# Two gaps between the operands of the first layer: where columns and weights begin in SBUF

## The chip, the cores and the metric

The kernel runs on one core of one Trainium2 chip. The metric is the device time of one execution in microseconds; the figure for a kernel is the median of its runs. One further execution is taken with the hardware profiler, and all views of the profile are of that one.

## What is computed

The reference first makes a short causal convolution over time (7 taps, weights from a softmax, one set of taps for each of 8 heads), and then a layer pair with a hard-swish between:

```python
out = np.einsum('hk,bskhg->bshg', w, x_unf)   # (8, 4096, 192), 7 taps
h = x @ w_in                                  # (32768, 192) @ (192, 2048)
relu6 = np.clip(h + 3.0, 0.0, 6.0)
g = h * relu6 / 6.0
return (g @ w_out).astype(np.float32)         # (32768, 2048) @ (2048, 192)
```

## The kernel before

The 32768 tokens are worked in 32 blocks of 1024 tokens. In each block the convolution gives `y`, the first layer gives `g`, and the second layer gives 192 outputs for each token. The work of the next block's convolution and of the sums for the second layer is laid between by hand (`tc.manual_schedule()`, with lists of jobs and due times), so the order on each engine is the order of the program.

**First layer.** A block's 1024 tokens are two groups of 512 columns; the 192 inputs are 3 thirds of 64 rows. Rows 0-63 of a tile hold the lower group, rows 64-127 the upper one. `y` is split into a high and a low part, `y_own[HIGH]` and `y_own[LOW]` (tiles `y0` and `y1`), and `swap_parts` copies them with DMAs of SP into `y_other`, where the two halves of the rows are exchanged. The weights are split in the same way into `w_in0` and `w_in1`. A product is made in three passes:

```python
PASSES = (HIGH, HIGH), (LOW, HIGH), (HIGH, LOW)   # (weights, columns)
```

One unit `n` of 16 makes 128 of the 2048 hidden features for both token groups: 3 passes x 3 thirds x 2 halves of the rows, 18 matmuls (`products`, L442), each 64 rows x 128 weight columns x 512 columns of `y`. The two matmuls of a pair stand in different halves of the array's rows. Units 0 to 7 read the own parts, units 8 to 15 the exchanged ones (in the first block they alternate). ScalarE (`relu`, L315) and VectorE (`gate`, L319) then turn a unit's two PSUM banks into `g`; four such pairs of banks go round.

In all this makes 32 blocks x 16 units x 9 pairs = 4608 pairs of matmuls. The operands are bitcast to float32r.

**Second layer.** It is a two-level Strassen-like scheme in plain float32, each matmul 128 rows x 32 weight columns x 512 or 256 columns, on four column groups of the array side by side (L582; the first block uses `direct_chunk`, L330, instead). `plain` puts a 512-column matmul at 2 units of a column group's list, `small` puts a 256-column one at 1 unit; at the point where the rest is added, the code asserts `clock[q] == 44`. Among its moving operands are `g`, sums of it (`s1`, `s3` and others), `z`, the early sums in the slots of `y0` and `y1` (`z0`, `z1`), and `z_other` in the slot of `y_other`. `pe_tap` (L923) makes a part of the first block's convolution on TensorE, with 128 x 128 weights.

**Places in SBUF.** A pool gives its tiles addresses one behind the other, in the order in which they are first asked for; pools stand in the order in which they are opened (`cst`, `xs`, `ys`, `yo`, `ot`, and others behind them). In `cst` stand, among others, `g`, then `w_in0`, `w_in1`, `w_out`; in `yo` stand `sm`, `y0`, `y1` and the tile with the tag `other`. In bytes in each partition, a third of `y` takes 2048, a part 6144, and the 128 weight columns of a matmul 512.

Of the kernel before, what the change touches and what calls it, by code (L numbers as in the profile page):

```python
# [11 lines left out]
F32 = mybir.dt.float32  # L12
# [8 lines left out]
HIGH, LOW = range(2)  # L21
# [10 lines left out]
def kernel(  # L32
# [9 lines left out]
    P = nc.NUM_PARTITIONS  # L42
# [6 lines left out]
    N = 512  # L49
# [3 lines left out]
    K3 = D // D2  # L53
# [7 lines left out]
    NP = NC // 2  # L61
# [5 lines left out]
    cst = ctx.enter_context(tc.tile_pool(name="cst", bufs=1))  # L67
    xs = ctx.enter_context(tc.tile_pool(name="xs", bufs=1))
    ys = ctx.enter_context(tc.tile_pool(name="ys", bufs=1))
    yo = ctx.enter_context(tc.tile_pool(name="yo", bufs=1))  # L70
# [48 lines left out]
    nc.vector.memset(zeros, 0.0)  # L119


    w_in_parts = [cst.tile([P, NP, K3, P], F32, name=f"w_in{n}") for n in range(2)]
    def own_tiles(name):
        return [yo.tile([P, K3, N], F32, name=f"{name}{n}", tag=f"y{n}") for n in range(2)]

    sm = yo.tile([P, 1], F32, name="sm")
    y_own, z_early = own_tiles("y"), []

    def other_tile():
        return yo.tile([P, 2, K3, N], F32, name="y_other", tag="other")  # L130

    y_other = [other_tile()]
    w_out = cst.tile([P, NP, 7, DH], F32, name="w_out")
    B11, B12, B21, B22, T1, T2, T4 = range(7)
# [99 lines left out]
    def r32(ap):  # L234
        return ap.bitcast(F32R)
# [39 lines left out]
    y = ys.tile([P, K3, N], F32, name="y")  # L275
# [26 lines left out]
    def swap(to, part):  # L302
        nc.sync.dma_start(out=to[D2:P], in_=part[0:D2])
        nc.sync.dma_start(out=to[0:D2], in_=part[D2:P])
# [118 lines left out]
    def high_of(out, x):  # L423
        nc.scalar.mul(r32(out), x, CUT)

    def low_of(out, x, high, engine):
        engine.tensor_tensor(out=r32(out), in0=x, in1=high, op=ALU.subtract)
# [3 lines left out]
    def swap_parts(thirds=slice(0, K3)):  # L431
        y_other[0] = other_tile()
        for n in range(2):
            swap(y_other[0][:, n, thirds], y_own[n][:, thirds])

    def products(n, slot, s, steps=range(3), begin=False, end=False):
        group, c = divmod(n, NP)
        for m_ in steps:
            wn, yn = PASSES[m_]
            for k in range(2):  # L440
                r = slice(k * D2, (k + 1) * D2)
                nc.tensor.matmul(  # L442
                    out=psum[:, 2 * slot + k], lhsT=r32(w_in_parts[wn][r, c, s]),
                    rhs=r32(y_other[0][r, yn, s] if group else y_own[yn][r, s]),
                    start=begin and m_ == 0, stop=end and m_ == 2, skip_group_check=True,
                )

# [14 lines left out]
    def first_layer(i, jobs):  # L462

        def unit(n):
            slot = free_slots.pop(0)
            for m_ in range(3):
                for s in range(K3):
                    products(n, slot, s, (m_,), s == 0, s == K3 - 1)
            to, both = places(n, slot)
            relu(to, both)  # L470
            gate(to, both)
            free_slots.append(slot)
# [50 lines left out]
    TH = N // 2  # L523
# [34 lines left out]
    def second_layer(i, between):  # L558
        last = i + 1 == NB
        ours = [free_slots.pop(0) for _ in range(3)]  # L560
        d, e, b, c, a, x_ = (psum[:, 2 * n + k] for n in ours for k in range(2))
# [87 lines left out]
        f, h = ends  # L649
# [2 lines left out]
        A2, B2, C2 = a[second, lo], a[third, lo], a[first, lo]  # L652
        T_2, T_4 = x_[second], e[first]
        A, B, V = f[fourth], h[fourth], b[fourth]
        z_other = yo.tile([P, 3, NP // 2, TH], F32, name="z_other", tag="other")
        sums_a12 = z_other[:, 0], z_other[:, 1], z_other[:, 2], z[:, :, 1]

        def sum_a12(n):
# [44 lines left out]
        t = clock[2]  # L703
# [204 lines left out]
    with tc.manual_schedule():  # L908
# [8 lines left out]
        thirds = [slice(s, s + 1) for s in range(K3)]  # L917
# [10 lines left out]
        b, b1 = (2 * free_slots[-1] + k for k in range(2))  # L928
# [14 lines left out]
        def thirds_of(n, *which, end=False):  # L943
            if n not in early:
                early[n] = free_slots.pop(0)
            for s in which:
                products(n, early[n], s, begin=s == pe_third, end=end)

        def high_y(s, of):
            high_of(y_own[HIGH][:, thirds[s]], of)  # L950
            swap(y_other[0][:, HIGH, thirds[s]], y_own[HIGH][:, thirds[s]])

        def low_y(s, of):
            low_of(y_own[LOW][:, thirds[s]], of, y_own[HIGH][:, thirds[s]], nc.vector)
            swap(y_other[0][:, LOW, thirds[s]], y_own[LOW][:, thirds[s]])

        def all_of(s):
            return y[:, thirds[s]]
# [7 lines left out]
        for u in conv0[5 : per - 3]:  # L966
            u()
        join(0)
        high_y(pe_third, psum[:, b : b + 1])
        part(0)  # L970
        for u in conv0[per - 3 : per]:
            u()
        low_y(pe_third, psum[:, b : b + 1])
        high_y(0, all_of(0))
        low_y(0, all_of(0))
        thirds_of(0, pe_third, 0)
        thirds_of(NP, pe_third)
        split(1)
        clamp(1)
        for u in conv0[per + 2 : per + 2 * pe_taps]:  # L980
            u()
        add(y[:, 1], psum[:, b1], y[:, 1])
        high_y(1, all_of(1))
        join(1)
        part(1)
        low_y(1, all_of(1))
        for n in (5, 6, 7, 8):
            load(n)
# [36 lines left out]
        for r in range(2 * NP):  # L1025
            k = order[r]
            if k in early:
                slot = early[k]
                if k == NP:
                    thirds_of(k, 1, end=True)  # L1030
            else:
                slot = free_slots.pop(0)
                for m_ in range(3):
                    for s in range(K3):
                        products(k, slot, s, (m_,), s == 0, s == K3 - 1)
            to, both = places(k, slot)
            relu(to, both)
            n = joins.get(r)
# [62 lines left out]
        begin_block_two()  # L1101
        direct_out(0, *third)
        swap_parts()
        w_sums(((T3, B22, B12),))
        last = ctx.enter_context(tc.tile_pool(name="last", bufs=1, reuse_waits="tile"))
# [6 lines left out]
        for i in range(1, NB):  # L1112
            jobs = dict(zip((3, 6, 9, 12), ([job] for job in conv[3:7])))
            jobs[-1] = left
            if i > 1 and conv:

                jobs[-1] = left[:2] + conv[1:2] + left[2:]
                jobs[1] = conv[2:3]
            first_layer(i, jobs)
            for job in conv[7:]:  # L1120
                job()
            conv = []

            def begin_conv():
                x_tiles[i + 2] = load_x(i + 2)
                conv.extend(conv_jobs(i + 2, True))

            between = []
            if i + 1 < NB:
                between = [(52.4, split_high), (63, split_rest), (64.2, swap_parts)]  # L1130
            if i + 2 < NB:
                between += [(40, begin_conv), (65, lambda: conv[0]())]
            left = second_layer(i, between)
# [33 lines left out]
```

## Time and profile before

| | |
|---|---|
| median of 3 runs | 2195.71 us (2195.3 to 2195.73) |
| the profiled execution | 2195.85 us |
| its span | 2194.1 us |
| granted TensorE clock | 1.00 |
| TensorE busy | 2185.0 us (100%), 23086 matmul records |
| VectorE busy | 1976.1 us (90%) |
| ScalarE, GpSimd busy | 1270.9 us (58%), 1012.9 us (46%) |

The span runs from the first to the last instruction that the profile shows. "PE" is TensorE's matmuls, "PEld" its weight loads, which run beside matmuls. Matmuls are pipelined: one recorded at 386 ns starts while those before it still run, so the pace is read from the distance of starts, not from the recorded length. The chain that ended last is followed back from the last instruction, at each step to what released it.

### The profile page before, as it was taken

Reading aid. Unit: us, or ns where it says so; the run is one execution under the profiler, and the core shown is the slowest. Engines: PE = TensorE matmul, PEld = TensorE weight load, DVE = VectorE, ACT = ScalarE, POOL = GpSimd, SP = SyncE. Lnnn points to the kernel's source line nnn. Section 1 sums busy time; section 2 is a strip of 40 time slices with the busy share of each in tenths; the row PEclk is TensorE's granted clock in tenths of the full one; section 3 lists DMA queues with packets and bytes.
Section 4 is the critical chain, followed back from the end, with each engine's and each line's share of the span. In section 5 each row is a group of like instructions: output and inputs, shape, how many; then the busy total and the mean of one; then the engine's idle time right before and its main releaser. Section 6 shows DMA issues by size and latency. Waiting matters only on the chain.

```text
span 2194.1 us, 53702 instructions
## 1 busy us (share of the span) xinstructions
PE 2185.0 (100%) x23086; PEld 1565.5 (71%) x23086; DVE 1976.1 (90%) x1871; ACT 1270.9 (58%) x1761; POOL 1012.9 (46%) x859
## 2 busy tenths in 40 slices
PE   9999999999999999999999999999999999999998
PEld 5577777777777777777777777777777777777776
DVE  8889899889899898998989988999989999999987
ACT  7456565565655665555656556565566565565654
POOL 3445543355433555334554335553355543455433
PEclk9999999999999999999999999999999999999999
DMA  7366556756567665666655675656666566755564
GB/s 166 66 119 100 97 99 111 128 90 107 97 111 121 103 109 92 109 112 121 98 97 100 112 126 91 106 97 113 120 107 106 91 109 112 122 96 97 100 104 63
DMA packets 329821, 231.80 MB, mean 106 GB/s; under 512 B 208816, under 2 KB 293296, under 8 KB 329584
## 3 DMA queue, kind: packets, MB, share of 16 engines
q0 software_dynamic: 98752, 122.35, 36.6%
q1 hardware_dynamic: 229320, 105.73, 23.9%
q8 instruction: 181, 2.97, 0.6%
q10 hardware_dynamic: 1512, 0.30, 0.1%
q14 instruction: 56, 0.46, 0.1%
HBM read 31.72 MB, written 25.17 MB: 26 GB/s over the span
## 4 chain that ended last, share of the span: by engine, by line
PE 99%; ACT 0%; DVE 0%; POOL 0%; issue 0%; POOLq 0%; DVEq 0%
PE psum L582 49%; PE psum L442 47%; PE psum L330 2%; PE psum L923 0%; PE psum L931 0%; ACT g L315 0%; DVE results L409 0%; POOL w_in L230 0%; ACT scale L207 0%; ACT sig L204 0%; POOL out_dram L356 0%; ACT sig L210 0%; POOL sig L221 0%; DVE xt L832 0%; ACT w_in L229 0%
## 5 line engine op out<-in xcount | busy, mean ns | idle before, releaser
L582 PE MATMUL psum<-g,w_out 128*32 128x512 f32 (+1 forms) x5720 | 1023.7, 508 | 0.0
L315 ACT ACTIVATE g<-psum,half 128x1024 f32<-128x1024 f32 x512 | 571.3, 1116 | 313.5 <-PE psum L442 311.3
L582 PE MATMUL psum<-s,w_out 128*32 128x512 f32 (+1 forms) x3272 | 735.6, 570 | 0.9 <-DVE results L409 0.9
L319 DVE SCALAR_TENSOR_TENSOR g<-g,psum 128x1024 f32<-128x1024 f32 x512 | 609.1, 1211 | 134.3 <-ACT g L315 133.9
L540 POOL TENSOR_TENSOR s<-g 128x256 f32<-128x256 f32 x248 | 257.2, 1037 | 750.9 <-DMA out_dram<-results 639.6
L582 PEld LDWEIGHTS psum<-g,w_out 128*32 128x32 f32 x5720 | 421.0, 110 | 171.5 <-issue 61.6
L442 PE MATMUL psum<-y,w_in 64*128 64x512 f32 x4608 | 534.3, 388 | 0.4
L442 PE MATMUL psum<-y_other,w_in 64*128 64x512 f32 x4608 | 528.7, 386 | 0.0
L442 PEld LDWEIGHTS psum<-y,w_in 64*128 64x128 f32 x4608 | 428.6, 184 | 120.9 <-issue 26.0
L442 PEld LDWEIGHTS psum<-y_other,w_in 64*128 64x128 f32 x4608 | 431.6, 184 | 90.7
L1006 DVE SCALAR_TENSOR_TENSOR y<-x,c_sb,y 128x1536 f32<-128x1536 f32 x156 | 305.1, 1956 | 1.9 <-ACT y L1003 1.8
L582 PEld LDWEIGHTS psum<-s,w_out 128*32 128x32 f32 x3272 | 227.5, 110 | 106.3 <-issue 54.0
L582 PE MATMUL psum<-g,w_s 128*32 128x256 f32 x1488 | 289.3, 379 | 0.0
L389 POOL TENSOR_TENSOR s<-g 128x1024 f32<-128x1024 f32 x93 | 236.9, 2715 | 0.4 <-DVE g L319 0.4
L582 PE MATMUL psum<-z,w_s 128*32 128x256 f32 x992 | 235.1, 380 | 0.0
L389 DVE TENSOR_TENSOR s<-g 128x1024 f32<-128x1024 f32 x124 | 187.5, 1531 | 1.1
L582 PEld LDWEIGHTS psum<-g,w_s 128*32 128x32 f32 x1488 | 149.9, 110 | 31.9
L582 PE MATMUL psum<-s,w_s 128*32 128x256 f32 x744 | 170.7, 379 | 0.0
L482 ACT ACTIVATE z<-g 128x512 f32<-128x512 f32 x186 | 142.5, 766 | 18.4 <-DVE g L319 18.4
L409 DVE TENSOR_TENSOR g<-g 128x1024 f32<-128x1024 f32 x124 | 143.6, 1219 | 1.1
L409 DVE TENSOR_TENSOR results<-psum,results 32x256 f32<-32x256 f32 (+2 forms) x221 | 107.9, 488 | 39.6 <-PE psum L582 34.2
L389 DVE TENSOR_TENSOR g<-g 128x2048 f32<-128x2048 f32 x62 | 139.4, 2286 | 1.0
(114 smaller groups left out, 2335.2 us busy)
## 6 DMA issues: line engine op xcount, KB each, us to landing
y_other<-y SPq DMA_DIRECT2D x124, 384.0 KB, 5.1
z<-g POOLq DMA_DIRECT2D x93, 512.0 KB, 5.6
z<-z POOLq DMA_DIRECT2D x62, 512.0 KB, 5.4
out_dram<-results SPq DMA_DIRECT2D x375, 64.0 KB, 2.6
y<-x POOLq DMA_DIRECT2D x30, 768.0 KB, 9.0
x<-in_x_dram SPq DMA_DIRECT2D x53, 388.5 KB, 7.3
g<-g POOLq DMA_DIRECT2D x31, 512.0 KB, 6.3
g<-in_moe_w_in_dram SPq DMA_DIRECT2D x16, 192.0 KB, 5.8
```

The lines of the kernel that those rows point to most:

```text
L315: nc.scalar.activation(r6, h, ACT.Relu, bias=half[:], scale=1.0 / 6.0)
L319: nc.vector.scalar_tensor_tensor(out=g_, in0=g_, scalar=1.0, in1=h, op0=ALU.min, op1=ALU.mult)
L330: lambda p=p: nc.tensor.matmul(out=bank[j * QS : (j + 1) * QS, tokens], lhsT=w_out[:, p, w, cols], rhs=x[:, p, tokens], start=(first and p ...
L389: engine.tensor_tensor(out=o[:, r], in0=a[:, r], in1=b[:, r], op=op)
L409: nc.vector.tensor_tensor(out=out, in0=x, in1=y, op=op)
L442: nc.tensor.matmul(out=psum[:, 2 * slot + k], lhsT=r32(w_in_parts[wn][r, c, s]), rhs=r32(y_other[0][r, yn, s] if group else y_own[yn][r, s ...
L482: nc.scalar.mul(to, x, sign)
L540: engine.tensor_tensor(out=o, in0=p, in1=q, op=op)
L582: nc.tensor.matmul(out=out, lhsT=w, rhs=x, start=start, stop=True, tile_position=(0, j * QS), skip_group_check=True,)
L1006: nc.vector.scalar_tensor_tensor(out=y[:], in0=taps_of(k), scalar=c_sb[:, k : k + 1], in1=y[:], op0=ALU.mult, op1=ALU.add,)
```

## The change

Empty tiles are put between the tiles that the first layer reads. A helper `gap` asks the pool for a tile of so many bytes in each partition and does nothing with it. Of its four uses two have a size: 64 bytes ahead of `y0`, and 256 bytes between `y1` and the tile with the tag `other`. Modulo 256, all columns then begin 64 bytes ahead of the weights; modulo 512 the own parts begin 320 bytes ahead and the exchanged parts 64. The shared tile becomes one row of words, of which `y_other` and `z_other` are views of the same sizes as before (`OTHER_GAP`, a distance between its two parts, is 0).

```diff
-    w_in_parts = [cst.tile([P, NP, K3, P], F32, name=f"w_in{n}") for n in range(2)]
+    def gap(pool, name, size):
+        if size:
+            pool.tile([P, size // 4], F32, name=name)
+
+    w_in_parts = [cst.tile([P, NP, K3, P], F32, name="w_in0")]
+    gap(cst, "gap_w", 0)
+    w_in_parts.append(cst.tile([P, NP, K3, P], F32, name="w_in1"))
...
     sm = yo.tile([P, 1], F32, name="sm")
-    y_own, z_early = own_tiles("y"), []
+    gap(yo, "gap_y0", 64)
+    y_own = [yo.tile([P, K3, N], F32, name="y0", tag="y0")]
+    gap(yo, "gap_y1", 0)
+    y_own.append(yo.tile([P, K3, N], F32, name="y1", tag="y1"))
+    z_early = []
+    gap(yo, "gap_other", 256)
+    OTHER_GAP = 0
+
+    def other_words(name):
+        return yo.tile([P, 2 * K3 * N + OTHER_GAP], F32, name=name, tag="other")
 
     def other_tile():
-        return yo.tile([P, 2, K3, N], F32, name="y_other", tag="other")
+        words = other_words("y_other")
+        return [
+            words[:, b : b + K3 * N].rearrange("p (s n) -> p s n", n=N)
+            for b in (0, K3 * N + OTHER_GAP)
+        ]
...
-            swap(y_other[0][:, n, thirds], y_own[n][:, thirds])
+            swap(y_other[0][n][:, thirds], y_own[n][:, thirds])
...
-                    rhs=r32(y_other[0][r, yn, s] if group else y_own[yn][r, s]),
+                    rhs=r32(y_other[0][yn][r, s] if group else y_own[yn][r, s]),
...
-        z_other = yo.tile([P, 3, NP // 2, TH], F32, name="z_other", tag="other")
+        z_other = other_words("z_other")[:, : 3 * NP // 2 * TH].rearrange(
+            "p (k u t) -> p k u t", u=NP // 2, t=TH
+        )
```

The two swaps of the first block (`high_y`, `low_y`) take the new views in the same way.

More of the change, by code (lines that the diff above doesn't have):

```diff
@@ L950, in high_y @@
             high_of(y_own[HIGH][:, thirds[s]], of)
-            swap(y_other[0][:, HIGH, thirds[s]], y_own[HIGH][:, thirds[s]])
+            swap(y_other[0][HIGH][:, thirds[s]], y_own[HIGH][:, thirds[s]])
         def low_y(s, of):
             low_of(y_own[LOW][:, thirds[s]], of, y_own[HIGH][:, thirds[s]], nc.vector)
-            swap(y_other[0][:, LOW, thirds[s]], y_own[LOW][:, thirds[s]])
+            swap(y_other[0][LOW][:, thirds[s]], y_own[LOW][:, thirds[s]])
         def all_of(s):
```

## The prediction

> **What bounds the kernel now.** I read the page first: which engine fills the span, and what the chain that ended last is made of.
>
> ```profile
> span 2194.1 us, 53702 instructions
> ...
> PE 2185.0 (100%) x23086; PEld 1565.5 (71%) x23086; DVE 1976.1 (90%) x1871; ACT 1270.9 (58%) x1761; POOL 1012.9 (46%) x859
> ...
> PE psum L582 49%; PE psum L442 47%; PE psum L330 2%; PE psum L923 0%; PE psum L931 0%; ACT g L315 0%; DVE results L409 0%; POOL w_in L230 0%; ACT scale L207 0%; ACT sig L204 0%; POOL out_dram L356 0%; ACT sig L210 0%; POOL sig L221 0%; DVE xt L832 0%; ACT w_in L229 0%
> ...
> L442 PE MATMUL psum<-y,w_in 64*128 64x512 f32 x4608 | 534.3, 388 | 0.4
> L442 PE MATMUL psum<-y_other,w_in 64*128 64x512 f32 x4608 | 528.7, 386 | 0.0
> ```
>
> The chain is matrix work throughout: 49% second layer (L582), 47% first layer (L442). The last two rows' idle figures, 0.4 and 0.0 us, say that the first layer waits for nobody. So only the pace of the matmuls counts. The chain in order of time gives it by stage:
>
> ```profile
> 229.91 32.86 PE psum L442 x288
> 262.77 34.61 PE psum L582 x304
> ```
>
> A first layer is 288 matmuls, that is 144 pairs (rows 0-63 and 64-127 of the array work side by side), in 32.86 us. The timeline of TensorE inside one (start, length, count) gives the pace of a pair:
>
> ```profile
> 779.73 6.51 PE L442 MATMUL psum<-y,w_in 64*128 64x512 f32 x56
> 786.08 4.24 PE L442 MATMUL psum<-y_other,w_in 64*128 64x512 f32 x36
> ```
>
> One matmul is recorded at 0.386 us, so 28 pairs on the own parts step by (6.51 - 0.386) / 27 = 0.2268 us, and 18 pairs on the exchanged parts by (4.24 - 0.386) / 17 = 0.2267. Same step, and the same relation of addresses: the change puts the own parts at 320 modulo 512 with a gap of 64, so they stand at 256 now, and the exchanged parts at 64 with 320 of gaps before them, so they too stand at 256. Every third, part and weight block is a multiple of 512 bytes long, so all 4608 pairs share this one relation.
>
> How low could a pair go? The other 512-column matmuls show it:
>
> ```profile
> 9.77 6.60 PE L923 MATMUL psum<-x,diag 128*128 128x512 f32 x15
> 30.87 3.64 PE L330 MATMUL psum<-g,w_out 128*32 128x512 f32 x32
> ```
>
> The L923 passes step by (6.60 - 0.592) / 14 = 0.429 us with a 128-column load beside each. They are plain float32, which the program issues as two such passes per matmul; I take a pass to run at half the pace of the first layer's, so a pair without disturbance would be 0.429 / 2 = 0.2146 us (an estimate). A pair now pays some 12.1 ns above it.
>
> Is that extra fixed? The start of a first layer says no. These are rows of the timeline of TensorE in narrow windows, each opening on one pair; only the start, the first number, is read:
>
> ```profile
> 769.62 0.50 PE L442 MATMUL psum<-y,w_in 64*128 64x512 f32 x2
> ...
> 769.96 0.62 PE L442 MATMUL psum<-y,w_in 64*128 64x512 f32 x3
> ...
> 770.20 0.62 PE L442 MATMUL psum<-y,w_in 64*128 64x512 f32 x4
> ...
> 770.42 0.62 PE L442 MATMUL psum<-y,w_in 64*128 64x512 f32 x3
> ...
> 770.66 0.62 PE L442 MATMUL psum<-y,w_in 64*128 64x512 f32 x3
> ...
> 770.89 0.62 PE L442 MATMUL psum<-y,w_in 64*128 64x512 f32 x4
> ...
> 771.12 0.39 PE L442 MATMUL psum<-y,w_in 64*128 64x512 f32 x2
> ...
> 771.34 0.61 PE L442 MATMUL psum<-y,w_in 64*128 64x512 f32 x3
> ```
>
> After the first step, which waits for its weights, the steps are 0.24, 0.22, 0.24, 0.23, 0.23 and 0.22 us: same form, same relation of addresses, nothing awaited, yet they move by some 10 ns before they settle at the lowest. So a pair's time depends on how the weight load falls against the columns streamed beside it.
>
> **The change, part by part.** It adds and removes no instruction: a gap is an allocation. The two new views of the shared tile (three-dimensional slices of one row of words) have the same sizes and strides. Moved by 64 bytes: the own parts, and the early sums in their slots. Moved by 320: the exchanged parts, z_other in their slot, and every pool opened after (results, s1, s3, z).
>
> *Second layer and first block's direct product: 0.* Here streams run at half pace. The L330 rows read weights that start 0, 128, 256 or 384 bytes from the columns modulo 512 (2688 bytes from chunk to chunk, 128 from one column group to the next), and the 32 records, four to a step, take (3.64 - 0.592 - 0.02) / 7 = 0.433 us a step with a slower first one; L923 has 0.429. Four offsets, one pace. Bounds: 34.61 us a layer against 80 steps of 0.429 (each column group's list is 44 + 16 + 4 + 16 units long, a 512-column matmul being two) is 34.3, which leaves 0.3 us to win, 31 times, so 9 us, and as much to lose; I take 0, by the L330 row.
>
> *DMAs, DVE, ACT, POOL: 0.* Sizes, queues and order stay, and PE hides them. The cover is thinnest on DVE:
>
> ```profile
> 1444.40:1477.20 32.80, 32.80 (x289) 26.86 (x288) 30.19 (x26) 22.56 (x23) 23.65 (x21) 1.00 0.47 70
> ```
>
> The third figure is DVE: 30.19 us of a 32.8 us first layer. If all 12.1 ns went, the layer would shrink by 144 x 0.0121 = 1.7 us to 31.1, still 0.9 above. Were that cover gone, PE would wait for the gate (L319), 0.9 us a layer at most by these rows, 28 us in all; I take 0.
>
> *First layer: the whole effect.* Unknown: the step at the new relation, since no row of this trace has another at this pace. Upper gain: the step falls to 0.2146, 4608 x 12.1 ns = 56 us. Upper loss: it rises to the highest of the settling steps, about 0.236 by the rows' hundredths, 4608 x 9.2 ns = 42 us. I take a gain of half the extra, 6 ns, so 4608 x 6 = 28 us. Reason: both readers now start at the same place modulo 256 and within a few ns of each other. The columns then pass at 512 / 227 = 2.3 a ns; with 64 bytes, 16 columns, of lead they start some 7 ns of stream away from the load instead of on top of it. It is half because the columns run faster than the load (128 weight columns, against 512 in the pair) and lap it, so that modulo 256 they meet again within the load, whatever the start.
>
> The Trainium skill (TensorE: Matmul & The Clock Gate, "Back-to-back issue gap") puts a warm 512-column matmul at 512 / 2.4 + 2.5 = 216 ns; by its figure the extra would be 11 ns a pair and the largest gain about 50 us. No run here shows that figure for a row pair.
>
> **Rivals.**
>
> *No change: 2195.7.* The extra is the price of loading weights in the same rows, wherever they lie: one path shared by load and columns. For it: the step is the same to the rows' resolution in all 32 blocks' own and exchanged parts, and the half-pace rows are blind to offsets. Against: the settling steps differ although the loads are alike; but phase alone may do that.
>
> The Trainium skill speaks for this outcome. Its page "TensorE: Matmul & The Clock Gate" ("Step-by-step: what each phase is for") says that columns and weights come through two independent read ports and that loading the next weights takes no read bandwidth from the running matmul; "SBUF — State Buffer" ("Who interferes with whom") adds that TensorE waits for no one. By that rule placement is worth 0. The settling steps do not agree with it as it stands, since they vary with nothing to wait for.
>
> *Slower: about 2220.* The present step is the lowest of those that the trace shows. If moving the columns acts like another phase of the load, the pairs settle at one of the others: from 769.96 to 771.12 five steps take 1.16 us, 0.232 each, 5.3 ns above, 4608 x 5.3 = 24 us. At 0.236 it is 42 us (2238). It decides once the step passes 0.2277 us (1 ns, 4.4 us in all). For it: the lead may only move a meeting that now falls on the idle edge, before the load has begun, into its middle. Against: nothing in the trace says that the steady state is the best address, only the best phase.
>
> *One half gains, the other loses* is part of these: own and exchanged parts differ by 256 modulo 512, and each is 2304 pairs.
>
> **How the numbers follow.** The sum is made on the profiled execution: 2195.85 us (span 2194.1, and 1.8 around it); the median is 2195.71, 0.1 lower, so it carries over. Forecast 2195.7 - 28 = 2168. Chances: faster 0.47, as both streams now start together and the extra is not fixed; slower 0.38, as phases with a larger extra are plainly there and the direction of the shift is argued, not shown; no change 0.15. A difference of 0.2%, 4.4 us, is about what a measurement of this kernel can tell from none. The faster case alone spans 2140 to 2191. The range reaches from 2143 (nearly all the extra gone) to 2224 (just past the mean settling step); left out are about 0.03 below and 0.15 above.
>
> **What would show it.** Right: the two timeline rows of L442 with steps near 0.220 us, the chain's L442 pieces near 32.0 us, L582 pieces still 34.61, and idle before L442 still near 0. "No change" leaves 0.2267; "slower" shows 0.230 or more with L582 unmoved. If own and exchanged steps differ, the relation modulo 512 counts. The prediction is wrong in kind if L582 moves by over 0.3 us a layer, or if the gate L319 appears among what PE waits for.

## The result, and the profile after

The changed kernel takes 2205.11 us (median of 5 runs, 2204.81 to 2205.49) against 2195.49 before (5 runs, 2195.0 to 2195.73): 1.0044 times as long, 95% interval 1.003 to 1.0059. It is slower by 9.6 us. The forecast was 28 us faster. The sign was wrong, and the range (2143 to 2224) held the time only because it took in the rival "slower".

The page of the changed kernel (the first layer is now L463, the second L603):

```profile
span 2203.0 us, 53702 instructions
...
PE 2194.6 (100%) x23086; PEld 1616.4 (73%) x23086; DVE 1966.3 (89%) x1871; ACT 1272.3 (58%) x1761; POOL 1015.5 (46%) x859
...
L463 PE MATMUL psum<-y,w_in 64*128 64x512 f32 x4608 | 539.4, 390 | 0.2
L463 PE MATMUL psum<-y_other,w_in 64*128 64x512 f32 x4608 | 534.5, 388 | 0.0
```

The same number of instructions, the same full engine, and still no idle time ahead of the first layer (0.2 and 0.0 us): nothing new is waited for. The chain in order of time shows which stage grew:

```profile
230.16 33.18 PE psum L463 x288
263.34 34.61 PE psum L603 x304
```

A first layer went from 32.86 to 33.18 us, a second layer stayed at 34.61. Over 31 layers that is 0.316 x 31 = 9.8 us (0.316 from the unrounded starts). The first block's first layer adds 0.6; the first matmul of it starts 0.9 us earlier in this execution and the last block's end is 0.5 shorter; together +9.0, the difference of the two spans (2203.04 and 2194.07). So the whole loss is the pace of the first layer's pairs. The timeline of TensorE has it:

```profile
299.82 14.82 PE L463 MATMUL psum<-y,w_in 64*128 64x512 f32 x128
```

64 pairs: (14.82 - 0.386) / 63 = 0.2291 us a step, against 0.2268 before. From the starts in the trace (the mean of 60 settled steps in each of 31 layers; steps in ns below are taken in this way, where nothing else is said) it is 226.67 ns before and 228.89 after, on own and exchanged parts alike. 4608 pairs at 2.2 ns more are 10.2 us.

Narrow windows, each opening on one settled pair, show how the two differ in kind (read the starts only):

```profile
785.79 0.40 PE L463 MATMUL psum<-y,w_in 64*128 64x512 f32 x2
...
786.02 0.41 PE L463 MATMUL psum<-y,w_in 64*128 64x512 f32 x2
...
786.25 0.41 PE L463 MATMUL psum<-y,w_in 64*128 64x512 f32 x2
...
786.48 0.40 PE L463 MATMUL psum<-y,w_in 64*128 64x512 f32 x2
```

A hundredth is too coarse for single steps, but the recorded length already varies. In the trace the steps of one layer read 226, 229, 232, 226, 229, 231, 226, 229, 232 ns and so on: three unlike steps in turn. Before, after the first five steps of a layer, every step was 226 or 227 ns to its end (one step of 228 in the 31 layers aside). Before, the pairs settle on one step; now they go round.

### The profile page after: what moved, and what is told of

Its sections match the earlier page's. It is cut to its first block, busy times and chain, and to the rows that moved or that the text cites. A ratio compares the mean times of both kernels' runs of the same rounds, so it can differ in the third digit from the quotient of the medians.

```text
span 2203.0 us, 53702 instructions
## 1 busy us (share of the span) xinstructions
PE 2194.6 (100%) x23086; PEld 1616.4 (73%) x23086; DVE 1966.3 (89%) x1871; ACT 1272.3 (58%) x1761; POOL 1015.5 (46%) x859
## 4 chain that ended last, share of the span: by engine, by line
PE 98%; ACT 1%; DVE 0%; POOL 0%; DMA 0%; issue 0%; POOLq 0%; DVEq 0%
PE psum L603 48%; PE psum L463 48%; PE psum L351 2%; PE psum L946 0%; PE psum L954 0%; ACT g L336 0%; DVE results L430 0%; DMA y_other<-y 0%; POOL w_in L251 0%; ACT scale L228 0%; ACT sig L225 0%; POOL out_dram L377 0%; ACT sig L231 0%; POOL sig L242 0%; DVE xt L855 0%
## 5 line engine op out<-in xcount | busy, mean ns | idle before, releaser
L603 PE MATMUL psum<-g,w_out 128*32 128x512 f32 (+1 forms) x5720 | 1023.7, 508 | 0.0
L603 PE MATMUL psum<-s,w_out 128*32 128x512 f32 (+1 forms) x3272 | 735.6, 570 | 0.9 <-DVE results L430 0.9
L603 PEld LDWEIGHTS psum<-g,w_out 128*32 128x32 f32 x5720 | 421.8, 110 | 170.8 <-issue 61.7
L463 PE MATMUL psum<-y,w_in 64*128 64x512 f32 x4608 | 539.4, 390 | 0.2
L463 PE MATMUL psum<-y_other,w_in 64*128 64x512 f32 x4608 | 534.5, 388 | 0.0
L463 PEld LDWEIGHTS psum<-y,w_in 64*128 64x128 f32 x4608 | 452.7, 184 | 101.7 <-issue 26.0
L463 PEld LDWEIGHTS psum<-y_other,w_in 64*128 64x128 f32 x4608 | 456.7, 184 | 71.1 <-DMA y_other<-y 0.5
L603 PEld LDWEIGHTS psum<-s,w_out 128*32 128x32 f32 x3272 | 227.5, 110 | 105.7 <-issue 53.7
L1029 DVE SCALAR_TENSOR_TENSOR y<-x,c_sb,y 128x1536 f32<-128x1536 f32 x156 | 299.6, 1920 | 1.9 <-ACT y L1026 1.8
L603 PE MATMUL psum<-g,w_s 128*32 128x256 f32 x1488 | 289.4, 379 | 0.0
L603 PE MATMUL psum<-z,w_s 128*32 128x256 f32 x992 | 235.1, 380 | 0.0
L603 PEld LDWEIGHTS psum<-g,w_s 128*32 128x32 f32 x1488 | 150.3, 110 | 31.7
L603 PE MATMUL psum<-s,w_s 128*32 128x256 f32 x744 | 170.7, 379 | 0.0
```

The costliest lines, as they stand in the source:

```text
L463: nc.tensor.matmul(out=psum[:, 2 * slot + k], lhsT=r32(w_in_parts[wn][r, c, s]), rhs=r32(y_other[0][yn][r, s] if group else y_own[yn][r, s ...
L603: nc.tensor.matmul(out=out, lhsT=w, rhs=x, start=start, stop=True, tile_position=(0, j * QS), skip_group_check=True,)
L1029: nc.vector.scalar_tensor_tensor(out=y[:], in0=taps_of(k), scalar=c_sb[:, k : k + 1], in1=y[:], op0=ALU.mult, op1=ALU.add,)
```

## The experiments

Theory R: the step is a matter of where the streamed columns begin relative to the weights, modulo 256, pair by pair. Rivals: A, something else in the moved addresses costs the time; S, the step is the same everywhere but at 0; and, for the cause, L: the load takes time from the stream, in proportion to its columns (the prediction too put the extra down to the load). "Place" below means bytes that the columns begin ahead of the weights, modulo 256.

**One half moved, one not.**

```diff
-    gap(yo, "gap_y0", 64)
+    gap(yo, "gap_y0", 0)
...
-    gap(yo, "gap_other", 256)
+    gap(yo, "gap_other", 64)
```

> Gap ahead of y0 0, gap ahead of the shared tile 64: own parts begin 0 bytes ahead of the weights modulo 256 (as before), exchanged parts 64 (as after). In the result a pair steps by 0.2267 us before and by a mean of 0.2289 after, on own and exchanged parts alike. Theory R (the step depends only on where the streamed columns begin relative to the weights, modulo 256, pair by pair): own pairs step at 0.2267, exchanged ones at 0.2289, half of the loss of 9.6 us, so about 2200.4. Theory A (a few wrong bytes anywhere, or the moved sums and results, cost the time): both halves step alike, 2205 or 2195.5.

```profile
773.64 14.73 PE L463 MATMUL psum<-y,w_in 64*128 64x512 f32 x128
788.14 14.21 PE L463 MATMUL psum<-y_other,w_in 64*128 64x512 f32 x122
```

The start of the second row less that of the first is 14.50 us for 64 own pairs, 0.2266 each; the 61 exchanged pairs step by (14.21 - 0.386) / 60 = 0.2304, and that has the change-over in it, whose first steps are 237 and 235 ns; settled, they are at 228.89, exactly after's step. So R: inside one layer of one kernel the step changes with the place. The time, 2202.21 us (1.003, 1.0019 to 1.0042), is 1.8 above the 2200.4 expected: a first layer is 63 ns longer than the middle between before and after, most of it from the change-over and from the last pair before the second layer (0.37 us there, 0.32 before, 0.33 after).

**The first gap alone.**

```diff
-    gap(yo, "gap_other", 256)
+    gap(yo, "gap_other", 0)
```

> The change without its second gap: own and exchanged parts both 320 bytes ahead of the weights modulo 512, so both 64 modulo 256. Theory R with 256 (only the place modulo 256 counts): both halves step at 0.2289 us and the kernel takes 2205, as with both gaps. Theory R with 512: the exchanged half differs from after's 0.2289.

2205.01 us (1.0044, 1.0027 to 1.0061), both halves at 228.89 ns. With both gaps the exchanged parts stood at 64 modulo 512 and here at 320: the same step, so the second gap does nothing, and the place counts modulo 256 as far as this pair of places shows it. (The kernels with 8 and 4 bytes below have `y1` 256 bytes further off than `y0`, modulo 512; at 8 bytes the steps are 233 or 234 ns through both.)

**Columns and weights moved together.**

```diff
+    gap(cst, "gap_ahead", 64)
     w_in_parts = [cst.tile([P, NP, K3, P], F32, name="w_in0")]
```

(with the other gaps at 0)

> No gap between the operands; 64 bytes ahead of w_in0, so weights and columns both move by 64 bytes and own and exchanged parts begin 0 bytes ahead of the weights modulo 256, as before. Theory R (the relation counts): both halves step at 0.2267 us and a first layer takes 32.86 us. Theory A (the place of the columns or of the weights itself counts, modulo 256): a step above 0.2267; 0.2289 if it is the columns' place alone.

```profile
229.50 32.86 PE psum L464 x288
262.37 34.61 PE psum L604 x304
```

Both halves at 226.67 ns, a first layer of 32.86 us as before, 2195.24 us beside 2195.3 for before on the same chip. The columns begin where after's own parts begin (480 modulo 512), and nothing is lost (one run each). So it is the relation, not the address, and A falls.

**Other places.** Three kernels with 32-byte gaps and two with offsets inside wider tiles, each with one place for the own parts and one for the exchanged.

```diff
-    gap(yo, "gap_y0", 64)
+    gap(yo, "gap_y0", 32)       # 128, 160
...
-    gap(yo, "gap_other", 256)
+    gap(yo, "gap_other", 64)
```

> Own parts 32 bytes ahead of the weights modulo 256, exchanged 96: two more points of the step as a function of the place. Theory R: each half has a step of its own between 0.2146 and 0.236 us. Theory S (the step is the same at every place but 0, where the pairs lock): both 0.2289. Theory A: both 0.2267 or both 0.2289.

> Own parts 128 bytes ahead modulo 256, exchanged 192. Theory R: own and exchanged steps differ from each other; if the meeting of load and columns costs least half a turn away, own is under 0.2267. Theory S: both 0.2289.

> Own parts 160 bytes ahead modulo 256, exchanged 224 (that is 32 behind). Theory R: a step of its own for each. Theory S: both 0.2289.

```diff
+    OWN_AT, OTHER_AT, PAD_WORDS = 2, 4, 64      # words; then 1, 63, 64
+
+    def own_tile(name, tag):
+        words = yo.tile([P, K3 * N + PAD_WORDS], F32, name=name, tag=tag)
+        return words[:, OWN_AT : OWN_AT + K3 * N].rearrange("p (s n) -> p s n", n=N)
```

> Places finer than a pool gives: own parts begin 8 bytes ahead of the weights modulo 256, exchanged 16. Measured so far by the place modulo 256: 0 bytes 0.2267 us a pair, 32 0.2333, 64 0.2289, 96 0.2333, 128 0.2325, 160 0.2343, 192 and 224 0.2333. Theory P (0 is a narrow place at which the pairs settle into an even step): 8 and 16 are already near 0.2333. Theory W (a wide dip about 0): 8 and 16 lie between 0.2267 and 0.2300. If either is under 0.2267, a faster kernel than before is at hand.

> Full loads, own parts 4 bytes ahead of the weights modulo 256, exchanged 4 behind (252). Place 8 gave 0.2333, 16 0.2317. Theory P (place 0 is a narrow place): both above 0.2267, 0.2300 or more. If either is under 0.2267 there is a faster kernel than before.

| place, bytes modulo 256 | step of a settled pair, ns |
|---|---|
| 0 | 226.67 |
| 4 | 238.55 |
| 8 | 233.33 |
| 16 | 231.67 |
| 32 | 233.33 |
| 64 | 228.89 |
| 96 | 233.33 |
| 128 | 232.45 |
| 160 | 234.33 |
| 192 | 233.33 |
| 224 | 233.33 |
| 252 (4 behind) | 229.96 |

The ends of the table, from the timeline of the last of these kernels:

```profile
780.31 17.42 PE L469 MATMUL psum<-y,w_in 64*128 64x512 f32 x144
797.57 12.82 PE L469 MATMUL psum<-y_other,w_in 64*128 64x512 f32 x110
```

At 4 bytes 72 pairs take 17.26 us from the first row's start to the second's, 0.2397 each with the layer's start in it; at 252 the step is (12.82 - 0.386) / 54 = 0.2303. One word ahead costs 12 ns a pair, one word behind 3. So S falls, and so does any smooth picture: 0 is a single point among those tried, and the best of the twelve; 64 is the second best; five of the twelve give the same 233.33. An even step is not yet a low one: at 8 and at 192 bytes the steps settle at 233 or 234 ns each. Of the bounds set ahead, W's are missed at 8 and 16 bytes, P's only in part met (16 bytes is at 231.67, and 252 just under 230), and half a turn away, at 128, the step is not under 226.67. The kernels took 2224.61 (32 and 96), 2223.08 (128 and 192), 2226.96 (160 and 224), 2220.65 (8 and 16) and 2228.44 us (4 and 252), one run each; second layers stayed at 34.61 us in all five. None beats before.

**Shorter loads.** Does the load cost the stream its columns? From the second block on, with before's places or those of 32 and 96:

```diff
-                    out=psum[:, 2 * slot + k], lhsT=r32(w_in_parts[wn][r, c, s]),
+                    out=psum[0 : columns[0], 2 * slot + k],
+                    lhsT=r32(w_in_parts[wn][r, c, s, 0 : columns[0]]),
...
+        columns[0] = 64        # 32, 96
         for i in range(1, NB):
```

> Before's places. From the second block on each first-layer matmul loads 64 weight columns and not 128 (rows 0 to 63 of the banks are made; the other half of the features is left out, the relu reads old values there). Columns streamed as before. Theory L (the extra over 0.2146 is paid for each weight column loaded beside the stream): it halves, a pair steps at 0.2200 to 0.2207. Theory F (a fixed price for each pair of matmuls): 0.2267 stays.

> The same halving of the weight columns, with own parts 32 bytes ahead modulo 256 and exchanged 96, where a full pair steps at 0.2333 us. Theory L: the extra of 18.7 ns over 0.2146 halves, 0.2240 on both halves. Theory F: 0.2333 stays.

> Before's places; from the second block on the first layer loads 32 weight columns a matmul and not 128 (96 of 128 features left out). With 64 columns the step was 0.2300 us at place 0, 0.2308 and 0.2300 at places 32 and 96 where 128 columns gave 0.2333. Theory B (a pair costs 0.2267 by itself, with no load beside it; a load adds up to about 6.7 ns for 128 columns in proportion, and at place 0 nothing): 0.2267 to 0.2284. Theory L2 (0.2146 is the price without a load, and the load's cost is not in proportion): under 0.2230.

> 96 weight columns (32 features of 128 left out), own parts at place 0, exchanged at 64. At place 0: 128 columns 0.2267, 64 0.2300, 32 0.2317. Theory H: the longer the load, the lower the step at place 0, so 0.2283 on own (a line through the three); on exchanged between 0.2289 (128 columns) and 0.2317. Theory L (a load costs time by its columns): own at or under 0.2267.

| weight columns | place 0 | 32 | 64 | 96 |
|---|---|---|---|---|
| 128 | 226.67 | 233.33 | 228.89 | 233.33 |
| 96 | 230.00 | | 233.33 | |
| 64 | 230.00 | 230.81 | | 230.00 |
| 32 | 231.67 | 233.33 | | |

(The last figure is from the kernel with places 32 and 128 below, in 30 of its 31 layers.) At place 0 a shorter load makes the pair slower, not faster:

```profile
775.73 14.43 PE L443 MATMUL psum<-y,w_in 64*64 64x512 f32 x124
```

62 pairs with 64 columns: (14.43 - 0.386) / 61 = 0.2302. L and F both fall: no length of load tried brings a pair under 226.67 ns, let alone to the prediction's 0.2146. Elsewhere no order by length holds either: 64 columns are faster than 128 at places 32 and 96, and 96 slower at 64. Theory B, formed after the 64 columns (a bare pair at 0.2267), missed with the 32 columns as well (0.2317, above its 0.2284), and so did L2; the line of the kernel with 96 columns missed on both halves (230.0 against 228.3, and 233.33 against at most 231.7). The edit narrows the output of a matmul together with its load; the two were not told apart, and no kernel streams without a load.

**What the price belongs to.** With 32 columns, half of the tokens; then one row half alone, with 32 and with 128 columns:

```diff
-            for k in range(2):
+            for k in range(halves_made[0]):
...
-                    rhs=r32(y_other[0][r, yn, s] if group else y_own[yn][r, s]),
+                    rhs=r32(y_other[0][r, yn, s, t] if group else y_own[yn][r, s, t]),
...
+        columns[0], tokens_made[0], halves_made[0] = 32, 256, 2    # 32, 512, 1; 128, 512, 1
         for i in range(1, NB):
```

> 32 weight columns and 256 streamed columns in place of 512 (also half of the tokens left out, from the second block on). Where the 12 ns above half an L923 pass come from, if not from the load: Theory B1 (6% on each streamed column): a pair steps at 0.1133 to 0.1150 inside a unit. Theory B2 (a fixed price of about 13 ns for a pair): 0.1200 to 0.1217. Steps are read inside units only, since ScalarE and VectorE may now be late between them.

> 32 weight columns, 512 streamed columns, but only rows 0 to 63 of the array: the second matmul of each pair is left out from the second block on. Theory B3 (the price is that two streams run side by side in the two halves of the rows): a matmul steps at 0.2146 to 0.2160. Theory B1 or B2 (each stream has it alone): 0.2267 to 0.2284.

> Before's places, 128 weight columns, but only rows 0 to 63 of the array (the second matmul of each pair left out from the second block on). With 32 columns one row half stepped at 0.2314. Theory H1 (the even step comes from one stream and its own load): 0.2267. Theory H2 (it comes from the two halves side by side): 0.2300 or more.

256 streamed columns step at 116.3 ns on average inside units that wait for nothing, but that mean hides two paces: toward the end of a unit the steps are 113, 113, 114 ns in about a quarter of these units, 117, 118, 118 in about half, and mixed in the rest. The lower pace is half of 226.67 and within B1's bounds, the upper one 2.7 ns above them; neither is B2's 120. So the price goes with the streamed columns, not with the pair. This kernel waits for VectorE, and the granted clock then falls in places; there it shows more:

```profile
782.19 4.05 PE L444 MATMUL psum<-y,w_in 64*32 64x256 f32 x36 [0.77 <-DVE g L319]
```

The granted clock is 0.50 in this stretch, a matmul is recorded at 0.412 us, and 18 pairs step by (4.05 - 0.412) / 17 = 0.2140 us, in the trace 213 or 214 ns after the first step. By the clock alone 213.3 would be 106.7 ns at the full clock (an estimate), no more than a quarter of L923's 429 ns, where 113.3 was the least that held. So the extra is not a matter of TensorE's clock alone.

One row half with 32 columns steps at 231.67 ns, the same as the pair (the 0.2314 in the expectation above is a little low):

```profile
791.92 16.38 PE L444 MATMUL psum<-y_other,w_in 64*32 64x512 f32 x70
```

70 single matmuls, (16.38 - 0.39) / 69 = 0.2317. So a neighbour in the other half has no part in it (B3 falls, and B1's bounds are missed here by 3 ns). And with 128 columns one row half alone finds the low step:

```profile
786.10 16.48 PE L444 MATMUL psum<-y_other,w_in 64*128 64x512 f32 x72
```

72 single matmuls, (16.48 - 0.386) / 71 = 0.2267: H1. The low step is a matter of one stream and its own load.

**Does the place act through a long load only?**

> 32 weight columns a matmul (the other 96 of 128 features left out from the second block on), own parts 32 bytes ahead modulo 256, exchanged 128. With 128 columns these places gave 0.2333 and 0.2325 us, with 32 columns place 0 gave 0.2317. Theory H (the place acts only through a long load, which at place 0 holds the pairs in an even step; the column stream by itself takes about 0.2333 wherever it begins): with so short a load the place no longer matters, both halves within 0.2313 to 0.2333. Theory D (the place acts on any load): own and exchanged differ by over 1 ns from place 0's 0.2317 or from each other.

Own parts 233.33 ns in 30 of the 31 layers, exchanged 230.67: 2.7 apart, and the second is under H's bound. So D; the place acts even on a load a quarter as long, and H falls. The chain of this kernel shows more than was asked for:

```profile
163.04 33.05 PE psum L464 x288
...
230.71 33.53 PE psum L464 x281
```

Two first layers of one execution, the same instructions at the same addresses, and 0.48 us apart. The timeline says where (two layers, own parts then exchanged):

```profile
163.68 15.80 PE L464 MATMUL psum<-y,w_in 64*32 64x512 f32 x138
179.32 15.85 PE L464 MATMUL psum<-y_other,w_in 64*32 64x512 f32 x136
...
231.82 15.81 PE L464 MATMUL psum<-y,w_in 64*32 64x512 f32 x134
247.44 15.86 PE L464 MATMUL psum<-y_other,w_in 64*32 64x512 f32 x136
```

69 own pairs in 15.64 us, 0.2267 each; in the later layer 67 own pairs in 15.62 us, 0.2331. The first steps differ (252, 227, 226, 227 ns in the one; 256, 234, 230, 228 in the other), and the own parts then stay in what they fell into. Only that one layer of the 31 found the low step there. So the place alone does not set the price of a pair. It seems to decide which sequences of steps the pairs can fall into, and the way the layer begins which of them they do; the runs agree with this and do not prove it. At place 0 with full loads all 31 layers of before come to the low step within six pairs.

## Why the prediction was wrong

**The step that failed** is the first layer's term: "I take a gain of half the extra, 6 ns". Measured: a loss of 2.2 ns. Two readings under it were wrong. The first was the floor. 0.2146 us was half of an L923 pass, on the assumption that this stream runs at twice that pace when undisturbed; no kernel here came below a steady 0.2267 for 512 columns, with 128 columns of load or 32, with two row halves or one. So at none of the twelve places was any of the 12.1 ns to be had. The second was the cause. The unlike steps at the start of a layer were read as a matter of phase between load and stream, which the runs fit without showing it; but then place 0 was taken for the place where the two meet worst, and of the twelve it is where they settle best. The same rows held the warning: the settled step was the lowest of those that followed the first pair in that layer.

**The rival that came true** is "slower", in kind: the pairs no longer settle at the low step. It was priced by the mean of the settling steps, 5.3 ns a pair; place 64 cost 2.2, so 10 us and not 24, and its 0.2289 is under the 0.230 that the prediction named as this rival's sign. Its chance was 0.38. Most of the other places would have cost what it said or more (233.33 is 6.7 ns above).

**"No change"** falls with the first experiment: 226.67 and 228.89 ns side by side in one layer. The rule of the Trainium skill that stood behind it ("SBUF — State Buffer", "Who interferes with whom": TensorE waits for no one) does not cover what is measured here: no engine waits for another, yet TensorE's two operands disturb each other's pace by their addresses. The Trainium skill's 216 ns for a warm 512-column matmul in isolation ("TensorE: Matmul & The Clock Gate", "Back-to-back issue gap") was reached by no settled float32r step here; 226.67 is the least that held.

**What held.** The second layer's term of 0: 34.61 us before and after, and within 0.01 us in the kernels with other places, although s1, s3 and z moved too; streams at half pace do not mind the place. No wait took the place of another. Own and exchanged parts behave alike at 320 and 64 modulo 512, so the second gap had no part in it. The accounting by pairs, 4608 times the change of a step, gives 10.2 us, against 9.0 by which the spans differ; the start and the end of the execution take the difference back.

**What stays open** is what in the machine makes the stream lose its 6% to 11% over the 0.2146 us of the estimate, and why the relation of addresses steers it. The runs show that it goes with streamed columns, that one stream and its own load are enough for it, that a layer can keep the pace it fell into, and, in one kernel at place 0, that no such extra is left at half of the granted clock. They do not show the mechanism.

## What to carry to other kernels

Where TensorE is the bound, its operands may stand in a good relation by chance: adding or removing any small tile ahead of one of them can cost more than the edit it belongs to (here 32 bytes cost 6.7 ns in 227, and 4 bytes 12). That the steps are even does not tell it, since even steps of 226.67 and of 233.33 were both seen; the number does. Read the settled step of the matmuls before and after every change of the allocation, and hold the relation with a gap when tiles come or go. A step above a computed ideal is not by that a sum to be won: look first whether any row reaches the ideal at that pace.

## What was not expected of the hardware

- The steady step of 512 float32r columns depends on where the columns begin relative to the weights, modulo 256: 226.67 to 238.55 ns over twelve places, with 4 bytes enough for 12 ns. Moving both by 64 bytes changes nothing.
- Steps that do not settle go round in a fixed order (226, 229, 232 ns at place 64), and one execution can hold two regimes at one place: 226.7 and 233.3 ns in two layers with 32-column loads, 113.3 and 117.7 ns in units with 256 streamed columns.
- A pair with 256 streamed columns took 213.3 ns at half of the granted clock and 113.3 ns at the least at the full one: 1.88 times, not twice.
- A load of 96, 64 or 32 columns gave a longer step at place 0 (230.0, 230.0, 231.7 ns) than one of 128 (226.7).
- Plain float32 passes, at half the pace, kept a second layer at 34.61 us at every place tried.
